# The first factor of a two-factor Fourier transform, on sums and differences of pairs of rows

## Chip, core and metric

The kernel runs on one core of a Trainium2 chip. The metric is device time in microseconds (us) of one execution, as the median of several. Engines are named as the profile does: PE (matmul), PEld (its weight loads), DVE (VectorE), ACT (ScalarE), POOL (GpSimd), SP (the queue that issues most DMAs).

## What is computed

The reference mixes a sequence in the frequency domain, and puts the result through a small network:

```python
X = np.fft.rfft(x, axis=1)                 # x: (8, 3008, 256)
y = np.fft.irfft(X * (filt_r + 1j * filt_i)[None], n=3008, axis=1)
h = y.reshape(24064, 256) @ w_in           # (256, 2048)
g = np.where(h > 0, h, np.exp(np.minimum(h, 0)) - 1)
out = g @ w_out                            # (2048, 256)
```

All is float32.

## The kernel before

The transform of length 3008 = 47 x 64 is split in two factors. A row of x has the number n = 47 n2 + n1, with n2 from 0 to 63 and n1 from 0 to 46. The first factor goes over n2 and yields, for each n1, the frequencies k2 from 0 to 31 (real input needs no more); a second, short factor goes over n1. Rows n1 = i and n1 = 47 - i are handled together, so i runs from 0 to 23 (`H`), in six chunks of four (`NXC`, `XC`).

For each of the 8 batches (b), these units follow each other:

- `x_load(b, c)` brings a chunk of x (partitions 0 to 63: n2 for n1 = i; 64 to 127: n2 for n1 = 47 - i) and a chunk of the table `ta` of cosines and sines, 128x128 for each i. The table has four groups p of 32 outputs: the real and imaginary parts of the sum over both n1.
- `a_unit(b, c)` is the first factor: four matmuls (L173), one for each i, with the 128x128 table as weights and 256 columns of x. Two of them fill one PSUM bank; ACT copies it out (L174).
- `z_write` puts the result into a scratch tensor z in DRAM (L186), `z_read(b, g)` fetches it in another order (L190, L191): the second factor needs i on partitions, for four k2 at a time.
- `b_unit(b, g)` does the second factor on four 64-wide tiles of the array (`tile_mm`, L218), multiplies by the filter on DVE, and adds on POOL. `bi_unit`, `y_write`, `y_read` and `n_unit` are the way back to rows of y; `n_unit` (L275) ends with combinations on DVE.
- The network follows in quads: one batch has 6 groups m of rows and 4 quarters q of the 2048 hidden columns, so 24 quads a batch and 192 in all. `up_steps` and `down_steps` do the two products with seven block products in place of eight, both for weights (prepared once by `w_convert`) and for data. `mm` is L323, the products of the down side L405, DVE's additions out of PSUM (`add`) L331.
- `c_unit` and `o_unit` combine and transpose the output, and 24 DMAs a group write it.

Each engine takes its instructions in the order in which they are written out. The network is the frame: a loop runs over the quads, with the steps of up (U) and down (D) interleaved by hand, and two places in each quad where the units of the transform are put in. Place 0 is in the middle, after the first seven steps, and place 1 at the end. The table `plan` says what goes where. Batch b's first factor runs during batch b-1's quads:

```python
for c, s in enumerate((0, 2, 3, 4, 6, 7)):
    at(t + s, 0, a_unit, b, c)
    nb, nxt = (b, c + XBUFS) if c + XBUFS < NXC else (b + 1, c + XBUFS - NXC)
    if nb < B:
        at(t + s, 0, x_load, nb, nxt)
    at(t + s, 0, z_write, b, c)
```

Here t is the first quad of batch b-1. Four PSUM banks (`bank`) rotate among all units; in the middle of a quad one of them is held by an open sum ("s"), and the next that is asked for is that of the products 7 and 4 ("d", written phd in the profile). DVE's addition of L331 reads that bank after product 7; product 4 is added to the same bank after that.

Batch 0 has no network to hide behind. It runs first, in a section of its own ("boot"), together with the fetch and conversion of the weights: x for all six chunks, the filter (`f_read_first`), 16 weight pieces (`w_fetch` on POOL's queue, `w_convert` on DVE and ACT). `wait_x` holds POOL's queue until a chunk of x has come.

Of the kernel before, what the change touches and what calls it, by code (L numbers as in the profile page):

```python
# [10 lines left out]
FP32 = mybir.dt.float32  # L11
U32 = mybir.dt.uint32
AXT = mybir.ActivationFunctionType
# [8 lines left out]
N = 3008  # L22
# [12 lines left out]
XBUFS = 4  # L35
FBUFS = 3
LO, HI = slice(0, 48), slice(64, 112)


def _make_tables():  # L40

    n2, k2 = np.arange(N2), np.arange(K2)
    ta, tn = np.zeros((P, H, P)), np.zeros((P, H, P))  # L50
    for i in range(H):
        for h in range(2):
            if h and i == 0:
                continue
            n1 = N1 - i if h else i
            th = 2 * np.pi * (((N1 * n2[:, None] + n1) * k2[None]) % N) / N
            c, s = np.cos(th), -np.sin(th)
            c[:, 0], s[:, 0] = 1.0, 1.0 - 2.0 * (n2 % 2)
            sign = -1.0 if h else 1.0
            r = slice(h * 64, h * 64 + 64)  # L60
            for p, v in enumerate((c, sign * s, s, sign * c)):
                ta[r, i, p * 32:p * 32 + 32] = v
                tn[p * 32:p * 32 + 32, i, r] = v.T
    i = np.arange(H)[:, None]
    gb, gr, gi = (np.zeros((P, 2, 64)) for _ in range(3))
    q = np.arange(N1)[None]
    th = 2 * np.pi * ((i * np.where(q < 24, q, 70 - q)) % N1) / N1
    c, s = np.cos(th), np.sin(th)
    sign = np.where(q < 24, 1.0, -1.0)
    gb[0:24, 0, :N1], gb[24:48, 0, :N1] = c, s  # L70
    gb[64:88, 0, :N1], gb[88:112, 0, :N1] = c * sign, -s * sign
    for o in (0, 64):
        gr[o:o + N1, 0, 0:24], gr[o:o + N1, 0, 24:48] = 2 / N * c.T, 2 / N * s.T
        gi[o:o + N1, 0, 0:24], gi[o:o + N1, 0, 24:48] = 2 / N * (c * sign).T, -2 / N * (s * sign).T
    k1 = np.arange(24)[None]
    t0 = 2 * np.pi * ((i * k1) % N1) / N1
    t3 = 2 * np.pi * ((i * (32 + 64 * k1)) % N) / N
    c0, s0, c3, s3 = np.cos(t0), np.sin(t0), np.cos(t3), np.sin(t3)
    gb[0:24, 1, 0:24], gb[24:48, 1, 24:48] = c0, c3
    gb[64:88, 1, 24:48], gb[88:112, 1, 0:24] = -s3, -s0  # L80

    m0, m3 = np.full((24, 1), 2 / N), np.full((24, 1), 2 / N)
    m0[0] = m3[23] = 1 / N
    s0[:, 0] = s3[:, 23] = 0.0
    gr[0:24, 1, 0:24], gr[24:48, 1, 24:48] = m0 * c0.T, m3 * c3.T
    gi[0:24, 1, 24:48], gi[24:48, 1, 0:24] = -m0 * s0.T, -m3 * s3.T
    return [t.astype(np.float32) for t in (ta, tn, gb, gr, gi)]
# [8 lines left out]
def kernel(  # L96
# [18 lines left out]
    glob = pool("glob", 1)  # L115
    xp = pool("xp", XBUFS)
    tap = pool("tap", XBUFS)
    tnp = pool("tnp", 2)
    t1p = pool("t1p", 3)
    t2p = pool("t2p", 2)  # L120
# [16 lines left out]
    junk = glob.tile([P, 1], FP32, name="junk")  # L137
    fd = fdp.tile([NG, 2, 48, 2, 2, D], FP32, name="fd")

    xs, tas, tns, t1s, t2s, ss, t3s, t4s, zs, yds, ys, g_of, po_of, cs_ = ({} for _ in range(14))  # L140

    def raw(src, row, ap, col=0):
        return bass.AP(tensor=src.tensor, offset=src.offset + row * D + col, ap=ap)
# [9 lines left out]


    def x_load(b, c, queue=nc.sync, place=None):
        t, w = place or (xp.tile([P, XC, D], FP32, tag="xc", name="xc"), tap.tile([P, XC, P], FP32, tag="ta", name="ta"))
        xs[b, c], tas[b, c] = t, w
        skip = 1 if c == 0 else 0
        if skip:
            nc.gpsimd.memset(t[64:P, 0, :], 0.0)  # L160
        queue.dma_start(w, ta_d[:, ts(c, XC), :])
        lo = b * N + c * XC
        nc.sync.dma_start(t[0:64], raw(x, lo, [[N1 * D, 64], [D, XC], [1, D]]))
        hi = b * N + N1 - c * XC - skip
        nc.sync.dma_start(t[64:P, skip:XC, :], raw(x, hi, [[N1 * D, 64], [-D, XC - skip], [1, D]]))

    def a_unit(b, c):
        t = t1s[b, c] = t1p.tile([P, XC, D], FP32, tag="t1", name="t1")
        xt, w = xs.pop((b, c)), tas.pop((b, c))
        for r in (0, 2):  # L170
            k, ps = bank("psa")
            for u in range(2):
                nc.tensor.matmul(ps[:, u, :], w[:, r + u, :], xt[:, r + u, :], start=True, stop=True)  # L173
            nc.scalar.activation(out=t[:, r:r + 2, :], in_=ps, func=AXT.Copy)  # L174
            banks.append(k)

    def z_write(b, c):  # L180
        if c == 0:
            zs[b] = zp.tile([96, K2 + 1, D], FP32, tag="z", name="z")
        t = t1s.pop((b, c))
        for p in range(4):
            r0 = p * H + c * XC
            nc.sync.dma_start(zs[b][r0:r0 + XC, 0:K2, :].rearrange("n k d -> k n d"), t[p * 32:p * 32 + 32, :, :])  # L186

    def z_read(b, g):
        t = t2s[b, g] = t2p.tile([P, 4, D], FP32, tag="t2", name="t2")
        nc.sync.dma_start(t[LO], zs[b][0:48, 4 * g:4 * g + 4, :])  # L190
        nc.sync.dma_start(t[HI], zs[b][48:96, 4 * g:4 * g + 4, :])  # L191

    def f_read(b, g):
        t = fbufs[(b * NG + g) % FBUFS]
# [3 lines left out]
    def f_read_first(t, a):  # L198
# [3 lines left out]
        for c, src in enumerate((filt_r, filt_i)):  # L202
# [7 lines left out]
                                            [[64 * D, n], [-4 * D, NG - g0], [1, D]]))  # L210
            if a == 0:
                nc.gpsimd.dma_start(t[24:48, 0, c, 0, :], raw(src, 32, [[64 * D, 24], [1, D]]))

    def tile_mm(ps, table, k, rhs, special):
        for u, w, v in ((0, 1, 1), (1, 1, 0)) if special else ((0, 2, 0),):
# [319 lines left out]
    with tc.manual_schedule():  # L537
# [3 lines left out]
        with tc.tile_pool(name="boot", bufs=1) as bp:  # L541
            ff = bp.tile([P, NG, 2, 2, D], FP32, name="ff")
            wbufs += [bp.tile([P, 2, 2, D], FP32, name="wb%d" % i) for i in range(2)]
            more = [(bp.tile([P, XC, D], FP32, name="xb%d" % i), bp.tile([P, XC, P], FP32, name="tb%d" % i))
                    for i in range(NXC - XBUFS)]

            def wait_x(c):

                nc.gpsimd.tensor_copy(out=junk[0:1], in_=xs[0, c][0:1, 0, 0:1])

            for k in range(2):
                w_fetch(k)
            for c in range(NXC):
                x_load(0, c, nc.scalar, more[c - XBUFS] if c >= XBUFS else None)
            nc.gpsimd.memset(ff, 0.0)
            for t, d in ((gb, gb_d), (gr, gr_d), (gi, gi_d)):
                nc.gpsimd.dma_start(t, d)
            w_convert(0)
            w_convert(1)
            wait_x(3)  # L560
            w_fetch(2)
            w_fetch(3)
            wait_x(5)
            for a in range(2):
                f_read_first(ff, a)
            for k in range(4, 7):
                w_fetch(k)
            for c in range(NXC):
                a_unit(0, c)
                z_write(0, c)  # L570
            for k in range(2, 6):
                w_convert(k)
                w_fetch(k + 5)
            z_read(0, 0)
            z_read(0, 1)
            for g in range(NG + 2):
                if g >= 2:
                    bi_unit(0, g - 2)
                if g < NG:
                    b_unit(0, g, ff[:, g])  # L580
                    if g + 2 < NG:
                        z_read(0, g + 2)
                if g >= 2:
                    y_write(0, g - 2)
                if g in CONVERTS:
                    w_convert(CONVERTS[g])
                if g == 1:
                    w_fetch(11)
                if g == 4:
                    w_fetch(12)  # L590
                if g in (5, 6):
                    x_load(1, g - 5)
# [26 lines left out]
        for b in range(B):  # L619
            t = (b - 1) * PER  # L620
            if b > 0:
                for c, s in enumerate((0, 2, 3, 4, 6, 7)):
                    at(t + s, 0, a_unit, b, c)
                    nb, nxt = (b, c + XBUFS) if c + XBUFS < NXC else (b + 1, c + XBUFS - NXC)
                    if nb < B:
                        at(t + s, 0, x_load, nb, nxt)
                    at(t + s, 0, z_write, b, c)
                for g in range(NG + 2):
                    s = t + 9 + g
                    if g >= 2:  # L630
                        at(s, 1, bi_unit, b, g - 2)
                    if g < NG:
                        at(s, 1, b_unit, b, g)
                    if g >= 2:
                        at(s, 1, y_write, b, g - 2)
                for g in range(NG):
                    s = t + 7 + g
                    at(s, 1, f_read, b, g)
                    at(s, 1, z_read, b, g)
            for m, (s, place) in enumerate(((20, 0), (25, 1), (29, 1), (32, 0), (36, 0), (40, 0))):  # L640
                if b > 0 or m > 0:
                    at(t + s - (1 if m == 0 else 2), 0, y_read, b, m)
                    at(t + s, place, n_unit, b, m)
                at(t + PER + 4 * m + 5, 0, c_unit, b, m)
                at(t + PER + 4 * m + 6, 0, o_unit, b, m)
# [54 lines left out]
```

## Time and profile before

| | |
|---|---|
| time, median of 3 | 2713.19 us (2712.85 to 2714.78) |
| span of the profiled execution | 2712.6 us, mean clock 0.978 |
| PE busy | 2618.7 us, 97% |
| DVE busy | 1809.0 us, 67% |
| L173, matmuls of `a_unit` (psa<-xc,ta; 16 more stand under psa<-xb,tb) | 368 records, 379 ns in the median |
| L174, copies of `a_unit` | 96, 584 ns mean |
| z<-t (L186) | 192 issues of 128 KB, 4.5 us to landing |
| t<-z (L190, L191) | 128 issues of 192 KB, 3.8 us to landing |
| ta<-ta_t on SP | 42 issues of 256 KB, 4.5 us to landing |

How to read it: busy time of PE is made of records that overlap in the pipe, so durations of groups are best taken from the start of one to the start of the next. A matmul statement in float32 appears as two records. DMA issues are named by destination and source. The time from issue to landing is the median.

### The profile page before, as it was taken

How to read it: one execution, taken by the hardware profiler on the slowest of the kernel's cores; microseconds unless marked ns; L12 is line 12 of the kernel's file. 1: busy time of each engine (PE TensorE's matmuls, PEld its weight loads, DVE VectorE, ACT ScalarE, POOL GpSimd, SP SyncE). 2: the span in 40 equal slices, each digit the busy share in tenths (PEclk: the TensorE clock that was granted, in tenths of full speed). 3: DMA queues.
4: the chain of work that ended last, by engine and by line, in shares of the span. 5: the costliest groups of instructions: out<-in, count | busy, mean ns of one | idle time of the engine just before them, and what ended most of it. 6: DMA issues, size and time to landing. Idle time of an engine off the chain costs nothing.

```text
span 2712.6 us, 35960 instructions
## 1 busy us (share of the span) xinstructions
PE 2618.7 (97%) x12992; PEld 2244.2 (83%) x12992; DVE 1809.0 (67%) x3147; ACT 1474.5 (54%) x2561; POOL 277.8 (10%) x325
## 2 busy tenths in 40 slices
PE   3689999999999999999999999999999999999998
PEld 1278878987899888998889887898789988899887
DVE  4866775667666676657765677666766667666765
ACT  2255555555555555555555555565555555555554
POOL 4311210002000120001200021000210012000000
PEclk7599999999999999999999999999999999999999
DMA  9655321434113431253313332143421233110010
GB/s 244 173 122 129 90 72 35 108 87 115 44 39 96 107 94 37 55 132 74 81 39 101 89 90 69 37 108 84 113 60 40 61 83 96 38 39 20 20 28 16
DMA packets 229424, 214.44 MB, mean 79 GB/s; under 512 B 131620, under 2 KB 192566, under 8 KB 229248
## 3 DMA queue, kind: packets, MB, share of 16 engines
q1 hardware_dynamic: 210592, 173.65, 25.7%
q0 software_dynamic: 17792, 36.93, 5.6%
q8 instruction: 103, 1.69, 0.3%
q10 hardware_dynamic: 864, 1.57, 0.2%
q14 instruction: 73, 0.60, 0.1%
HBM read 136.97 MB, written 78.12 MB: 79 GB/s over the span
## 4 chain that ended last, share of the span: by engine, by line
PE 95%; DMA 2%; DVE 1%; issue 1%; ACT 0%; POOL 0%; SPq 0%; DVEq 0%; ACTq 0%; POOLq 0%
PE po L405 42%; PE phs L323 24%; PE phd L323 12%; PE pha L323 6%; PE psn L275 3%; PE psa L173 3%; PE pva L218 2%; PE psr L218 2%; DMA wb<-in_moe_w_in_dram 1%; DMA tb<-ta_t 0%; DMA ff<-in_filt_i_dram 0%; PE pvb L218 0%; DMA ff<-in_filt_r_dram 0%; DMA xb<-in_x_dram 0%; DVE wm L488 0%
## 5 line engine op out<-in xcount | busy, mean ns | idle before, releaser
L405 PE MATMUL po<-g,wo 128*128 128x256 f32 (+1 forms) x5376 | 1293.4, 375 | 0.0
L405 PEld LDWEIGHTS po<-g,wo 128*128 128x128 f32 x5376 | 1019.5, 190 | 115.6
L334 ACT ACTIVATE g<-phs 128x512 f32<-128x512 f32 (+1 forms) x576 | 338.7, 588 | 844.5 <-PE phs L323 843.8
L331 DVE TENSOR_TENSOR g<-phd,g 128x512 f32<-128x512 f32 (+1 forms) x384 | 259.4, 675 | 537.9 <-ACT e L341 295.2
L341 ACT ACTIVATE e<-e 128x512 f32<-128x512 f32 (+1 forms) x768 | 477.0, 621 | 24.4
L323 PE MATMUL phs<-ys,wi 128*128 128x256 f32 (+1 forms) x1536 | 388.6, 375 | 11.2 <-ACT g L334 11.2
L323 PE MATMUL phs<-y,wi 128*128 128x256 f32 (+1 forms) x1536 | 394.8, 379 | 0.0
L345 DVE SCALAR_TENSOR_TENSOR g<-e,g 128x512 f32<-128x512 f32 (+1 forms) x576 | 386.6, 671 | 0.0
L340 ACT ACTIVATE e<-g 128x512 f32<-128x512 f32 (+1 forms) x576 | 352.9, 613 | 34.9 <-DVE g L331 30.1
L323 PEld LDWEIGHTS phs<-y,wi 128*128 128x128 f32 x1536 | 284.8, 190 | 82.9 <-ACT t L246 34.1
L323 PEld LDWEIGHTS phs<-ys,wi 128*128 128x128 f32 x1536 | 291.9, 190 | 45.5 <-ACT g L334 12.3
L345 DVE SCALAR_TENSOR_TENSOR g<-e,phs 128x512 f32<-128x512 f32 (+1 forms) x192 | 129.8, 676 | 138.6 <-ACT e L341 138.6
L235 POOL TENSOR_TENSOR sr<-sr,sp 128x512 f32<-128x512 f32 x64 | 81.1, 1267 | 1274.9 <-DVE sp L232 1274.9
L340 ACT ACTIVATE e<-phs 128x512 f32<-128x512 f32 (+1 forms) x192 | 112.9, 588 | 161.6 <-PE phs L323 161.6
L323 PE MATMUL phd<-ys,wi 128*128 128x256 f32 (+1 forms) x768 | 193.9, 375 | 0.5 <-DVE g L331 0.5
L323 PE MATMUL pha<-y,wi 128*128 128x256 f32 (+1 forms) x768 | 193.8, 375 | 0.0
L323 PE MATMUL phd<-y,wi 128*128 128x256 f32 (+1 forms) x768 | 193.7, 375 | 0.0
L323 PEld LDWEIGHTS phd<-ys,wi 128*128 128x128 f32 x768 | 145.7, 190 | 17.7 <-DVE g L331 1.3
L323 PEld LDWEIGHTS pha<-y,wi 128*128 128x128 f32 x768 | 145.8, 190 | 16.7 <-ACT y L277 0.2
L323 PEld LDWEIGHTS phd<-y,wi 128*128 128x128 f32 x768 | 145.8, 190 | 16.5
L385 DVE TENSOR_TENSOR g<-g,g 128x512 f32<-128x512 f32 (+1 forms) x192 | 130.7, 681 | 6.6
L382 DVE TENSOR_TENSOR g<-g,g 128x512 f32<-128x512 f32 (+1 forms) x192 | 130.7, 681 | 6.6
(102 smaller groups left out, 2313.2 us busy)
## 6 DMA issues: line engine op xcount, KB each, us to landing
z<-t SPq DMA_DIRECT2D x192, 128.0 KB, 4.5
t<-z SPq DMA_DIRECT2D x128, 192.0 KB, 3.8
yd<-t SPq DMA_DIRECT2D x128, 192.0 KB, 2.8
t<-yd SPq DMA_DIRECT2D x192, 128.0 KB, 3.7
xc<-in_x_dram SPq DMA_DIRECT2D x84, 256.0 KB, 5.2
f<-fd POOLq DMA_DIRECT2D x112, 192.0 KB, 3.7
out_dram<-o SPq DMA_DIRECT2D x640, 32.0 KB, 1.6
tn<-tn_t SPq DMA_DIRECT2D x48, 256.0 KB, 3.4
```

The lines of the kernel that those rows point to most:

```text
L173: nc.tensor.matmul(ps[:, u, :], w[:, r + u, :], xt[:, r + u, :], start=True, stop=True)
L218: nc.tensor.matmul(ps[:, u:u + w, :], table[k, v, :], rhs[k, u:u + w, :], start=True, stop=True)
L275: nc.tensor.matmul(ps[:, ts(q, P)], t[:, i - 4 * m, ds(dh * P, P)], w[:, i - 4 * m, :], start=True, stop=True)
L323: nc.tensor.matmul(ps[:, a, 0:h], w_in[q][:, COMBO[n], a, :], y[n], start=start and a == 0, stop=True, skip_group_check=True)
L331: nc.vector.tensor_tensor(out=g[o], in0=i0, in1=i1, op=ALU.add)
L334: nc.scalar.activation(out=g[o], in_=i0, func=AXT.Copy)
L340: nc.scalar.activation(out=e, in_=src, func=AXT.Relu, scale=-1.0)
L341: nc.scalar.activation(out=e, in_=e, func=AXT.Exp, scale=-1.0)
L345: nc.vector.scalar_tensor_tensor(out=g[n], in0=es[n], scalar=1.0, in1=src, op0=ALU.subtract, op1=ALU.max)
L382: nc.vector.tensor_tensor(out=b12, in0=b22, in1=b12, op=ALU.subtract)
L385: nc.vector.tensor_tensor(out=g["t4"], in0=g["b21"], in1=g["t2"], op=ALU.subtract)
L405: nc.tensor.matmul(po[i][:, u, 0:h], w_out[q][:, COMBO[n], a, :], g[n][:, a, :], start=q == 0 and a == 0 and n in (1, 3, 6, 4), stop=True, ...
```

## The change

A cosine or sine of the angle 2 pi (47 n2 + n1) k2 / 3008 keeps its value when n2 grows by 32 if k2 is even, and changes its sign if k2 is odd. So even k2 need only x[n2] + x[n2 + 32], and odd k2 only x[n2] - x[n2 + 32], with n2 from 0 to 31. The change has DVE make these sums and differences (`x_unit`), and lets the first factor run on a contraction of 32 rows for each n1. A 64x64 tile then holds both n1 of one i, and all four groups p for the 16 even, or the 16 odd, k2. Four such tiles fill the array: two i on the upper and lower rows, even and odd k2 on the left and right columns. Eight matmuls of 256 columns do a chunk.

Around it, the layout of x changes (partitions: 32 n2 of n1 = i, 32 n2 of 47 - i, for two halves of the chunk; the free dimension holds n2 and n2 + 32), the table halves, z has one row for each i with 128 lines in the order (p, k2) and one of padding, so that `z_write` takes two DMAs in place of four and `z_read` four in place of two. `x_unit` goes into place 0 of the quad before its `a_unit`. In the boot section the first factor stands ahead of the later weight fetches in the text, and the first two `w_convert` come after chunks 0 and 2.

```diff
+    tb = ta.reshape(2, 2, 32, NXC, 2, 2, 4, 16, 2)[:, 0].transpose(3, 0, 1, 2, 4, 7, 5, 6)
+    ta = np.ascontiguousarray(tb).reshape(P, H // 2, P)
...
+    sdp = pool("sdp", 2)
...
     def x_load(b, c, queue=nc.sync, place=None):
...
-        queue.dma_start(w, ta_d[:, ts(c, XC), :])
-        lo = b * N + c * XC
-        nc.sync.dma_start(t[0:64], raw(x, lo, [[N1 * D, 64], [D, XC], [1, D]]))
-        hi = b * N + N1 - c * XC - skip
-        nc.sync.dma_start(t[64:P, skip:XC, :], raw(x, hi, [[N1 * D, 64], [-D, XC - skip], [1, D]]))
+        queue.dma_start(w, ta_d[:, 2 * c:2 * c + 2, :])
+        for h in range(2):
+            i = XC * c + 2 * h
+            r = slice(64 * h, 64 * h + 32)
+            nc.sync.dma_start(t[r].rearrange("p k u d -> p k (u d)"),
+                              raw(x, b * N + i, [[N1 * D, 32], [32 * N1 * D, 2], [1, 2 * D]]))
+            r = slice(64 * h + 32, 64 * h + 64)
+            for u in range(2):
+                if i + u == 0:
+                    nc.gpsimd.memset(t[r, :, 0, :], 0.0)
+                else:
+                    nc.sync.dma_start(t[r, :, u, :],
+                                      raw(x, b * N + N1 - i - u, [[N1 * D, 32], [32 * N1 * D, 2], [1, D]]))
+
+    def x_unit(b, c):
+        t = xs[b, c]
+        u = sds[b, c] = sdp.tile([P, 2, D], FP32, tag="sd", name="sd")
+        nc.vector.tensor_tensor(out=u, in0=t[:, 0], in1=t[:, 1], op=ALU.add)
+        nc.vector.tensor_tensor(out=t[:, 1], in0=t[:, 0], in1=t[:, 1], op=ALU.subtract)
...
     def a_unit(b, c):
...
-        for r in (0, 2):
-            k, ps = bank("psa")
-            for u in range(2):
-                nc.tensor.matmul(ps[:, u, :], w[:, r + u, :], xt[:, r + u, :], start=True, stop=True)
-            nc.scalar.activation(out=t[:, r:r + 2, :], in_=ps, func=AXT.Copy)
-            banks.append(k)
+        (i0, p0), (i1, p1) = (bank("psa") for _ in range(2))
+        for u in range(2):
+            for o, src in ((0, sm), (64, xt[:, 1])):
+                for ps, r in zip((p0, p1), HALVES):
+                    nc.tensor.matmul(ps[o:o + 64, u, :], w[r, u, o:o + 64], src[r, u, :], start=True, stop=True)
+        nc.scalar.activation(out=t[:, 0:2, :], in_=p0, func=AXT.Copy)
+        nc.scalar.activation(out=t[:, 2:4, :], in_=p1, func=AXT.Copy)
+        banks.extend((i0, i1))
...
-            zs[b] = zp.tile([96, K2 + 1, D], FP32, tag="z", name="z")
+            zs[b] = zp.tile([H, 4 * K2 + 1, D], FP32, tag="z", name="z")
...
-        for p in range(4):
-            r0 = p * H + c * XC
-            nc.sync.dma_start(zs[b][r0:r0 + XC, 0:K2, :].rearrange("n k d -> k n d"), t[p * 32:p * 32 + 32, :, :])
+        z = zs[b][XC * c:XC * c + XC, 0:4 * K2, :].rearrange("i (q r) d -> r q i d", r=2)
+        for r in range(2):
+            nc.sync.dma_start(z[r], t[HALVES[r]])
...
-        nc.sync.dma_start(t[LO], zs[b][0:48, 4 * g:4 * g + 4, :])
-        nc.sync.dma_start(t[HI], zs[b][48:96, 4 * g:4 * g + 4, :])
+        for p, r in enumerate((0, 24, 64, 88)):
+            k = p * K2 + 4 * g
+            nc.sync.dma_start(t[r:r + 24].rearrange("i u d -> i (u d)"), zs[b][:, k:k + 4, :].rearrange("i u d -> i (u d)"))
...
-            w_convert(0)
-            w_convert(1)
...
+            for c in range(NXC):
+                x_unit(0, c)
+                a_unit(0, c)
+                z_write(0, c)
+                if c in (0, 2):
+                    w_convert(c // 2)
             for k in range(4, 7):
                 w_fetch(k)
-            for c in range(NXC):
-                a_unit(0, c)
-                z_write(0, c)
...
                 for c, s in enumerate((0, 2, 3, 4, 6, 7)):
+                    at(t + s - 1, 0, x_unit, b, c)
                     at(t + s, 0, a_unit, b, c)
```

More of the change, by code (lines that the diff above doesn't have):

```diff
@@ L37 @@
 LO, HI = slice(0, 48), slice(64, 112)
+HALVES = slice(0, 64), slice(64, 128)
 def _make_tables():
@@ L138 @@
     fd = fdp.tile([NG, 2, 48, 2, 2, D], FP32, name="fd")
-    xs, tas, tns, t1s, t2s, ss, t3s, t4s, zs, yds, ys, g_of, po_of, cs_ = ({} for _ in range(14))
+    xs, tas, tns, t1s, t2s, ss, t3s, t4s, zs, yds, ys, g_of, po_of, cs_, sds = ({} for _ in range(15))
     def raw(src, row, ap, col=0):
@@ L155, in x_load @@
     def x_load(b, c, queue=nc.sync, place=None):
-        t, w = place or (xp.tile([P, XC, D], FP32, tag="xc", name="xc"), tap.tile([P, XC, P], FP32, tag="ta", name="ta"))
+        t, w = place or (xp.tile([P, 2, 2, D], FP32, tag="xc", name="xc"), tap.tile([P, 2, P], FP32, tag="ta", name="ta"))
         xs[b, c], tas[b, c] = t, w
-        skip = 1 if c == 0 else 0
-        if skip:
-            nc.gpsimd.memset(t[64:P, 0, :], 0.0)
-        queue.dma_start(w, ta_d[:, ts(c, XC), :])
-        lo = b * N + c * XC
@@ L167, in a_unit @@
+    def x_unit(b, c):
[3 more added lines that the diff above has]
+        nc.vector.tensor_tensor(out=t[:, 1], in0=t[:, 0], in1=t[:, 1], op=ALU.subtract)
     def a_unit(b, c):
         t = t1s[b, c] = t1p.tile([P, XC, D], FP32, tag="t1", name="t1")
-        xt, w = xs.pop((b, c)), tas.pop((b, c))
-        for r in (0, 2):
-            k, ps = bank("psa")
-            for u in range(2):
-                nc.tensor.matmul(ps[:, u, :], w[:, r + u, :], xt[:, r + u, :], start=True, stop=True)
-            nc.scalar.activation(out=t[:, r:r + 2, :], in_=ps, func=AXT.Copy)
-            banks.append(k)
+        xt, w, sm = xs.pop((b, c)), tas.pop((b, c)), sds.pop((b, c))
+        (i0, p0), (i1, p1) = (bank("psa") for _ in range(2))
[6 more added lines that the diff above has]
+        banks.extend((i0, i1))
@@ L543 @@
             wbufs += [bp.tile([P, 2, 2, D], FP32, name="wb%d" % i) for i in range(2)]
-            more = [(bp.tile([P, XC, D], FP32, name="xb%d" % i), bp.tile([P, XC, P], FP32, name="tb%d" % i))
+            more = [(bp.tile([P, 2, 2, D], FP32, name="xb%d" % i), bp.tile([P, 2, P], FP32, name="tb%d" % i))
                     for i in range(NXC - XBUFS)]
             def wait_x(c):
-                nc.gpsimd.tensor_copy(out=junk[0:1], in_=xs[0, c][0:1, 0, 0:1])
+                nc.gpsimd.tensor_copy(out=junk[0:1], in_=xs[0, c][0:1, 0, 0, 0:1])
             for k in range(2):
```

## The prediction

> **What bounds the kernel now.** I read the page from the top: busy shares and slices, then the chain that ended last, then busy time by stretch.
>
> ```profile
> PE 2618.7 (97%) x12992; PEld 2244.2 (83%) x12992; DVE 1809.0 (67%) x3147; ACT 1474.5 (54%) x2561; POOL 277.8 (10%) x325
> PE   3689999999999999999999999999999999999998
> DVE  4866775667666676657765677666766667666765
> DMA  9655321434113431253313332143421233110010
> PE 95%; DMA 2%; DVE 1%; issue 1%; ACT 0%; POOL 0%; SPq 0%; DVEq 0%; ACTq 0%; POOLq 0%
> ```
>
> ```profile
> 0.00:68.00 68.00, 20.61 (x60) 13.24 (x60) 28.02 (x55) 15.70 (x26) 30.91 (x49) 0.74 1.03 244
> 68.00:136.00 68.00, 45.41 (x152) 16.13 (x149) 58.13 (x103) 17.70 (x32) 25.85 (x26) 0.51 0.64 174
> 272.00:2644.00 2372.00, 2372.00 (x11915) 2052.27 (x11914) 1593.76 (x2757) 1335.66 (x2320) 198.09 (x225) 1.00 0.28 71
> ```
>
> The columns of the second block are the stretch, its length, busy us of PE, PEld, DVE, ACT and POOL, the clock, the DMA share and GB/s. From 272 to 2644 us PE is busy for 2372.00 of 2372 us at full clock. There every nanosecond taken from PE comes off the total, and nothing else does, as long as no new wait opens. The first 68 us are another kernel: PE 20.6 us, DMA share 1.03, so transfers set the pace; from 68 to 136 DVE is busy for 58 of 68 us.
>
> Next, how long PE is held by one `a_unit`, and by the unit in this kernel that already has the shape of the new one, `b_unit`. From the timeline of PE (start, length, line, group):
>
> ```profile
> 521.80 1.89 PE L173 MATMUL psa<-xc,ta 128*128 128x256 f32 x8
> 523.53 0.92 PE L405 MATMUL po<-g,wo 128*128 128x224 f32 x4
> ...
> 608.20 1.89 PE L405 MATMUL po<-g,wo 128*128 128x256 f32 x8
> 610.01 0.64 PE L218 MATMUL psr<-t,gb 48*64 48x512 f32 x1
> 610.02 0.64 PE L218 MATMUL psi<-t,gb 48*64 48x512 f32 x1
> ...
> 611.03 1.13 PE L323 MATMUL phs<-y,wi 128*128 128x256 f32 x4
> 612.00 1.03 PE L323 MATMUL pha<-y,wi 128*128 128x256 f32 x4
> 612.87 1.03 PE L405 MATMUL po<-g,wo 128*128 128x256 f32 x4
> ```
>
> One matmul statement leaves two records. Lengths overlap (the pipe), so I go by starts: the four statements of `a_unit` take 523.53-521.80 = 1.73 us, 0.43 us for 256 columns. Four full-array records (two statements) step by 612.87-612.00 = 0.87.
>
> `b_unit` has four statements on 64-column tiles, two row halves by two column halves, 512 columns each. One after the other that is 4 x 0.87 = 3.5 us. The group before should have ended at 608.20+1.73 = 609.93; the group after starts at 611.03 and is 0.10 longer than usual (0.97 against 0.87). So it costs 1.10+0.10 = 1.20 us: the four tiles run together in 0.87, and 0.33 us goes into leaving and re-entering the full array. The `b_unit` of g = 0, where half of the tiles get two statements of 256 columns, comes out at 1.22 by the same sum (594.88+1.73 to 597.73, plus 0.11).
>
> Last, the gap of DVE in which the new work must fit, from its timeline in the quad that has `c_unit` too:
>
> ```profile
> 535.09 0.38 DVE L421 TENSOR_TENSOR c<-k,k 128x224 f32<-128x224 f32 x1
> 537.19 0.69 DVE L331 TENSOR_TENSOR g<-phd,g 128x512 f32<-128x512 f32 x1 [1.72 <-ACT e L341]
> 537.79 0.68 DVE L345 SCALAR_TENSOR_TENSOR g<-e,g 128x512 f32<-128x512 f32 x1
> ```
>
> and the table loads of the first 68 us, by queue (packets, MB, share of 16 engines):
>
> ```profile
> q10 hardware_dynamic: 864, 1.57, 9.1%
> ```
>
> **What the Trainium skill says.** TensorEngine Tiling (Array Packing), Key Properties: tiles of a 64x64 split load and multiply independently of each other, and changing the tiling mode drains the engine. The trace agrees: four tiles in 0.87 us, and 0.33 us for the change of mode. The same page, Gotcha 1: different row tiles must write to different PSUM banks; the new code does so (p0 for the upper half, p1 for the lower). VectorE: DVE Perf Modes, the perf-mode tier table: fp32 `tensor_tensor` has no fast mode. The trace has 0.68 us for 128x512, and 0.60 from start to start. DMA: Bandwidth & Descriptors, on why a DMA increments its semaphore by 16: a transfer is spread over the largest number up to 16 that divides its slowest dimension. By that rule a read of 24 rows uses 12 engines where 48 rows used 16; no view here shows it.
>
> **The change, part by part.**
>
> 1. *Matmuls of `a_unit`.* Four full-array statements of 256 columns become eight 64x64 ones, in two rounds of four different tiles. If the rounds run as in `b_unit`: 2 x 0.43 = 0.87 us of streaming, plus 0.33 for the mode, plus some 0.02 for more statements, so 1.22 us instead of 1.73. Saved: 0.51 us. Bounds: 1.03 us if half of the switch hides (0.70 saved), 1.40 if the sixteen short weight loads (129 ns each at L218) don't all hide (0.33 saved). I take 1.22 because L218 is the same engine, tile shape, type and neighbours. 48 units exist; six belong to the start, and the first of batch 1 (138.5 us) is followed by a wait of 9.36 us of PE that DVE's weight conversion sets. That leaves 41 on the path: 41 x 0.51 = 20.9 us.
>
> 2. *`x_unit` on DVE.* 48 pairs of 128x512 fp32 operations, 0.60 us apart: 1.2 us a pair (1.36 by lengths). It is queued in the middle of a quad, one quad (13 us) before its `a_unit`, so PE does not wait for it directly. Behind it in DVE's queue stands the addition of L331 out of phd, which PE needs before it may add product 4 into the same bank. DVE stands idle there for 5.76 us in a quad without extras and 1.72 us in the fullest one of steady state (1.43 in the narrowest that I found); all hold 1.2 us. If it were late by a little, PE has two more groups (0.87 each) between product 7 and product 4. On the path: 0.
>
> 3. *Transfers of steady state.* `x_load` goes from three to seven issues (six for the first), the table from 256 to 128 KB, `z_write` from four to two, `z_read` from two to four. SP issues at 0.3 to 0.6 us each; per batch this is some 24-12+16 = 28 more, about 13 us in a batch of over 300 us. x is asked for three quads or more before use, and the last `z_write` has two quads before its `b_unit`. DMA share is 0.28 in this stretch. On the path: 0.
>
> 4. *ACT.* Two copies of 128x512 a unit as before; the first becomes ready later, by under a microsecond, while ACT is still at the exponentials queued before it. On the path: 0.
>
> 5. *The start.* Six table loads shrink by half: 9.1% of 68 us is 6.2 us of all 16 engines, so 3.1 us of a saturated stretch are freed. Against it: 35 instead of 12 x issues on SP (some 0.42 us each, 15 us, where the old ones with their stalls took until 18.7 us), 1.2 us for sums before each matmul, and reads of z over fewer engines. The packets of x halve from 4 to 2 KB in one part, with no more bytes. The two early weight conversions move behind the first sums, into a time in which DVE had gaps of 8.84 and 14.44 us. The chain goes x, filter loads, weight fetch, conversion, so it should move up nearly by what is freed. I take -2.5 us, bounds -5 and +6.
>
> Sum: 2713.2 - 20.9 - 2.5 = 2689.8, say 2690.
>
> **The rivals.**
>
> A. *The start gives something back.* Many small issues on a saturated SP queue, and z read over 12 engines. For it: SP stalls between x loads already (issues at 2.07 and 5.52). Against: fewer bytes, half the z issues. 2713.2-20.9+6 = 2698.
>
> B. *The switch hides more than in `b_unit`.* 1.03 us a unit, start -5: 2713.2-28.7-5 = 2680. Against: all `b_unit`s that I measured pay the 0.33.
>
> C. *Tiles pair up but don't run four at a time*, for instance because four different moving operands are read at once: 2 x 0.87 + 0.33 = 2.07 us, 0.34 more than now, 41 x 0.34 = 14 us: about 2725 with the gain at the start. Slower than before. Against: `b_unit` reads two moving tiles on each row half too.
>
> D. *DVE becomes late.* If the addition out of phd slips past its slack by half a microsecond in each of the 41 quads, the gain is gone: 2711 to 2714. Against: the gaps above.
>
> **How the numbers follow.** Forecast 2690: 0.63. A: 0.15. B: 0.11. C: 0.06. D: 0.05. The range 2681 to 2700 takes in the forecast with the bounds of a unit from 1.1 to 1.3 us, all of A and nearly all of B; C and D stay out. Faster by over 0.2% (below 2707.8): forecast, A, B, and a part of D, 0.91; within: 0.02; slower: 0.07.
>
> **What would show it.** In the changed profile PE stays at full busy time from 272 us to the end of steady state; between the groups around an `a_unit` some 1.2 us pass, with eight tile records starting within some tens of nanoseconds and the second eight about 0.2 to 0.4 us later; `x_unit` shows 96 operations at 0.68 us, with the wait of L331 for phd shorter by 1.2 us, and no PE wait for DVE. The first `b_unit` starts near 62 instead of 64.0 us. It is wrong if the tile records start one pair after the other, if PE shows waits for DVE L331, or if the first `n_unit` (130.76 us) starts later than before.

## The result, and the profile after

The changed kernel takes 2698.05 us (median of 4, 2697.19 to 2699.75), the kernel before beside it 2713.72 us (4 runs, 2712.85 to 2714.78): ratio 0.9943, 95% interval 0.9926 to 0.9960. It is faster by 15.7 us where 23.4 were forecast, and lands on the number of rival A, 2698, though in part by luck (below). A second measurement in the middle of the experiments (below, the changed kernel again) gave 2698.47 us, ratio 0.9941 (0.9927 to 0.9954).

From the page of the changed kernel, the busy time of each engine:

```profile
PE 2593.4 (96%) x13376; PEld 2196.4 (81%) x13376; DVE 1870.0 (69%) x3243; ACT 1474.7 (55%) x2561; POOL 279.9 (10%) x325
```

PE lost 25.3 us of busy time, and DVE gained 61.0 us with 96 operations more. By stretch (start and end, length, busy us of PE, PEld, DVE, ACT and POOL, clock, DMA share, GB/s):

```profile
0.00:68.00 68.00, 12.90 (x97) 8.52 (x98) 32.08 (x64) 14.58 (x25) 30.49 (x48) 0.75 0.91 232
68.00:136.00 68.00, 44.02 (x146) 14.38 (x145) 58.07 (x101) 16.75 (x30) 25.92 (x26) 0.50 0.56 157
272.00:2630.00 2358.00, 2358.00 (x12222) 2016.81 (x12221) 1643.22 (x2832) 1339.52 (x2325) 199.19 (x225) 1.00 0.28 70
```

From 272 us on PE is as full as before, at full clock, so the frame of the prediction holds. In the first 68 us the DMA share is 0.91, where it was 1.03. Now one `a_unit` in the timeline of PE (start, length, group):

```profile
509.83 0.92 PE L426 MATMUL po<-g,wo 128*128 128x224 f32 x4
510.59 0.92 PE L344 MATMUL phs<-ys,wi 128*128 128x224 f32 x4
511.44 0.43 PE L194 MATMUL psa<-sd,ta 64*64 64x256 f32 x2
511.45 0.43 PE L194 MATMUL psa<-xc,ta 64*64 64x256 f32 x2
511.71 0.38 PE L194 MATMUL psa<-sd,ta 64*64 64x256 f32 x2
...
512.15 0.38 PE L194 MATMUL psa<-xc,ta 64*64 64x256 f32 x2
512.47 1.02 PE L426 MATMUL po<-g,wo 128*128 128x224 f32 x4
513.33 0.92 PE L344 MATMUL phd<-y,wi 128*128 128x224 f32 x4
```

Such a group of 224 columns holds PE for 0.76 us (510.59-509.83). The next group could have started at 511.35; it starts at 512.47 and takes 0.10 longer (513.33-512.47 = 0.86). So the unit costs 1.12+0.10 = 1.22 us, the number of the forecast. Its sixteen records start within 0.71 us (511.44 to 512.15), in four rounds of four, where the prediction had two rounds of eight.

To split the result I use one fixed point: a wait of PE for ACT of 9.4 us at the end of the weight conversions, which both kernels have once. It ends at the second line of each pair here (before, then after); the first line of each is a short wait just ahead of it:

```profile
137.63 1.02 PE L323 MATMUL phs<-ys,wi 128*128 128x224 f32 x4 [0.63 <-ACT g L334]
154.58 1.86 PE L323 MATMUL phs<-ys,wi 128*128 128x224 f32 x4 [9.36 <-ACT g L334]
141.60 1.02 PE L344 MATMUL phs<-ys,wi 128*128 128x224 f32 x4 [0.63 <-ACT g L355]
158.05 1.86 PE L344 MATMUL phs<-ys,wi 128*128 128x224 f32 x4 [9.37 <-ACT g L355]
```

From this release to the end: before 2712.6-154.58 = 2558.0 us, after 2697.7-158.05 = 2539.65. Steady state gained 18.4 us; all before the release lost 18.4-15.7, that is 2.7 us. The release itself comes 3.5 us later (158.05-154.58), and the trace of the second measurement gives 18.9 and 3.4 by the same two sums, so the loss is about 3 us.

Between the two waits the changed kernel gains: 16.95 us before, 16.45 after. The first `a_unit` of batch 1 stands there, and the chain that ended last runs through it. So this unit saves its 0.50 us too, which the prediction had put at nothing because a long wait follows, and what comes ahead of it lost some 3.2 us.

The waits of PE from 141 to 2630 us, in the changed kernel (engine, what waits, for what: us in total, times, longest):

```profile
PE phs L344 <- ACT g L355: 11.2, 3, 9.4
PE phd L344 <- DVE g L352: 1.8, 1, 1.8
```

The second was 0.5 us before. DVE's timeline shows where it is, in quad 5, while the second batch's first factor runs:

```profile
215.56 0.91 DVE L690 MEMSET f<- 128x1024 f32 x1 [0.16 <-issue]
...
217.95 0.38 DVE L442 TENSOR_TENSOR c<-k,k 128x224 f32<-128x224 f32 x1
218.25 0.69 DVE L182 TENSOR_TENSOR sd<-xc 128x512 f32<-128x512 f32 x1
218.97 0.69 DVE L183 TENSOR_TENSOR xc<-xc 128x512 f32<-128x512 f32 x1
219.58 0.69 DVE L352 TENSOR_TENSOR g<-phd,g 128x512 f32<-128x512 f32 x1
```

and PE's line for the group that waits, with the idle time and its releaser in brackets, before and after:

```profile
216.01 1.13 PE L323 MATMUL phd<-ys,wi 128*128 128x256 f32 x4 [0.48 <-DVE g L331]
220.32 1.13 PE L344 MATMUL phd<-ys,wi 128*128 128x256 f32 x4 [1.82 <-DVE g L352]
```

Three memsets, four operations of `c_unit` and the pair of `x_unit` stand in one queue with hardly a gap, and the addition of L352 that PE needs comes behind them.

At the start, the chain of waits of the changed kernel up to the first `b_unit` (start, length, what; `SPq` is an issue by SP):

```profile
12.13 0.31 SPq L176
...
12.96 0.42 SPq L169
...
22.37 0.43 SPq L176
22.84 6.09 DMA xb<-in_x_dram
...
29.06 0.17 POOL junk L570
...
33.13 11.07 DMA ff<-in_filt_i_dram
...
47.36 13.09 DMA z<-t
...
61.16 6.42 DMA t<-z
```

and that of the kernel before:

```profile
4.19 13.34 DMA tb<-ta_t
...
17.54 6.96 DMA xb<-in_x_dram
...
24.62 0.17 POOL junk L549
...
28.86 13.24 DMA ff<-in_filt_i_dram
...
51.30 8.03 DMA wb<-in_moe_w_in_dram
```

Before, the chain runs through transfers. After, 10.7 us of it are SP issuing x loads one after the other, 0.47 us from one to the next; the last chunk arrives at 29.06 us in place of 24.62, and GpSimd's fetches of the filter stand behind it. The chains go on differently, too, to the first filter product of `b_unit` on DVE. Before, the way is a fetch of weights (51.30+8.03 = 59.33) and the conversions behind it, which leave DVE at 68.45 us; the product follows at 69.04. After, the way is a write and a read of z (47.36+13.09, then 61.16+6.42 = 67.58) and the matmuls of `b_unit`; the product follows at 72.36. The first `n_unit` starts at 133.91 us, not 130.76.

### The profile page after: what moved, and what is told of

It is laid out like the page before. It is cut to its first block, busy times and chain, and to the rows that moved or that the text cites. A ratio compares the mean times of both kernels' runs of the same rounds, so it can differ in the third digit from the quotient of the medians.

```text
span 2697.7 us, 37154 instructions
## 1 busy us (share of the span) xinstructions
PE 2593.4 (96%) x13376; PEld 2196.4 (81%) x13376; DVE 1870.0 (69%) x3243; ACT 1474.7 (55%) x2561; POOL 279.9 (10%) x325
## 3 DMA queue, kind: packets, MB, share of 16 engines
q1 hardware_dynamic: 216096, 168.15, 25.3%
## 4 chain that ended last, share of the span: by engine, by line
PE 94%; DMA 2%; DVE 2%; issue 1%; SPq 0%; ACT 0%; POOL 0%; ACTq 0%; DVEq 0%; POOLq 0%
PE po L426 42%; PE phs L344 25%; PE phd L344 12%; PE pha L344 6%; PE psn L296 3%; PE pva L239 2%; PE psr L239 2%; PE psa L194 2%; DMA z<-t 0%; DMA ff<-in_filt_i_dram 0%; DMA ta<-ta_t 0%; PE pvb L239 0%; SPq L176 0%; DMA t<-z 0%; DMA xb<-in_x_dram 0%
## 5 line engine op out<-in xcount | busy, mean ns | idle before, releaser
L352 DVE TENSOR_TENSOR g<-phd,g 128x512 f32<-128x512 f32 (+1 forms) x384 | 259.6, 676 | 462.8 <-ACT e L362 277.8
```

The costliest lines, as they stand in the source:

```text
L352: nc.vector.tensor_tensor(out=g[o], in0=i0, in1=i1, op=ALU.add)
```

## Experiments

The ratios are against the kernel before, measured beside each run.

**1. Only the tiles undone.** The loads, the sums, the half tables and the scratch lines stay; the matmuls are full-array again. Even and odd k2 are not kept apart in it, so it doesn't compute the transform.

```diff
-            for o, src in ((0, sm), (64, xt[:, 1])):
-                for ps, r in zip((p0, p1), HALVES):
-                    nc.tensor.matmul(ps[o:o + 64, u, :], w[r, u, o:o + 64], src[r, u, :], start=True, stop=True)
+            for ps, src in ((p0, sm), (p1, xt[:, 1])):
+                nc.tensor.matmul(ps[:, u, :], w[:, u, :], src[:, u, :], start=True, stop=True)
```

> The changed kernel with its sums and differences, tables of half the size, loads and scratch lines, but with the first factor's matmuls over the full 128 partitions again: four a unit, of 128x128 weights over 256 columns. This leaves out part of the computation: even and odd k2 are not kept apart, so the output is not the transform. Theory (the tiles bring the whole gain in the steady stretch, 0.51 us times 41 units on the path): 2698.3 + 20.9 = 2719, so 5 us above the kernel before, which is what the rest of the change costs (x_unit, more issues, the start). Rival (the loads, tables or scratch lines bring a part of the gain): less than 2711. Rival (the tiles bring more than that and the rest of the change costs more): above 2724.

Measured: 2719.46 us (before 2714.53), ratio 1.0020 (1.0012 to 1.0028). One unit in the timeline of PE:

```profile
503.15 0.59 PE L193 MATMUL psa<-sd,ta 128*128 128x256 f32 x2
503.58 0.59 PE L193 MATMUL psa<-xc,ta 128*128 128x256 f32 x2
...
504.88 0.92 PE L425 MATMUL po<-g,wo 128*128 128x224 f32 x4
```

It takes 504.88-503.15 = 1.73 us again, and the total is 21.0 us over that of the changed kernel (2698.47), where 41 x 0.51 = 20.9 was forecast. So the tiles bring the whole gain. Between the two waits of the fixed point 16.95 us pass again (142.09 to 159.04), as before the change. The rest of the change costs 4.9 us: from the release of the 9.4 us wait (159.04 us) to the end (2719.0) 2560.0 us pass, 2.0 more than before, and 2.9 come before the release. That agrees with the changed kernel's 2.7.

**2. `x_unit` with its sum made three times** (batches 1 to 7).

```diff
         nc.vector.tensor_tensor(out=u, in0=t[:, 0], in1=t[:, 1], op=ALU.add)
+        if b > 0:
+            nc.vector.tensor_tensor(out=u, in0=t[:, 0], in1=t[:, 1], op=ALU.add)
+            nc.vector.tensor_tensor(out=u, in0=t[:, 0], in1=t[:, 1], op=ALU.add)
```

> The changed kernel with the sum of x_unit made three times for the seven later batches: 1.3 to 1.4 us more of DVE for each of 42 units, 57 us in all. Theory (DVE has a gap of 1.4 us or more before it answers TensorE, except in the quads with a c_unit or a memset, where 0.39 us is left beside some 1.7 us of TensorE's own slack): the time grows by 0 to 8 us, the wait of TensorE for the DVE addition of group d appears in the quads with x_unit and c_unit, and nowhere else. Rival (DVE is on the path wherever x_unit runs, and the 1.2 us of x_unit are paid each time): 30 to 57 us more, so over 2728.

Measured: 2709.25 us, ratio 0.9981 (0.9974 to 0.9988): 10.8 us more than the changed kernel, for 57.6 us more of DVE (1927.6 against 1870.0). The waits of PE from 141 to 2630 us:

```profile
PE phs L347 <- ACT g L358: 10.6, 2, 9.4
PE phd L347 <- DVE g L355: 7.2, 8, 3.3
```

The wait for DVE is the one that theory names, eight times, and accounts for 5.4 us of the growth. More shows when the weight loads (PEld) wait for the same addition, here and in the changed kernel:

```profile
PEld phd L347 <- DVE g L355: 13.8, 16, 3.7
PEld phd L344 <- DVE g L352: 2.9, 3, 2.2
```

From one quad's first `pha` group to the next, the two kernels differ in the quads that have both `x_unit` and `c_unit`: by 0.80 us in quad 1 and 0.37 us in quad 5 of the 24, in each of the six later batches, and by 3.1 us in the quad 5 shown above, 1.7 of them at a lower clock (last section). That is 10.1 of the 10.8 us. So DVE's slack takes in nearly all of one `x_unit`, but not of twice that: a fifth of the added work is paid, a little more than expected.

**3. The first factors in pairs.** `x_unit` for both chunks at place 0, and both `a_unit` calls at place 1, of quads 2, 4 and 6.

```diff
-                for c, s in enumerate((0, 2, 3, 4, 6, 7)):
-                    at(t + s - 1, 0, x_unit, b, c)
-                    at(t + s, 0, a_unit, b, c)
+                for c, s in enumerate((2, 2, 4, 4, 6, 6)):
+                    at(t + s, 0, x_unit, b, c)
+                    if c % 2 == 0:
+                        continue
+                    at(t + s, 1, a_unit, b, c - 1)
+                    at(t + s, 1, a_unit, b, c)
...
```

> The changed kernel with the first factors of steady state in pairs: two a_units back to back at the end of quads 2, 4 and 6, both x_units in the middle of the same quad. If a change of tile mode costs 0.33 us a time, a pair pays it once: 3 x 7 = 21 fewer, 7 us under e5; and no x_unit stands in quad 5 behind the memsets, so the wait of 1.8 us of PE there goes: together 2689 to 2691. If the cost of 0.33 us belongs to each unit (weight loads that do not hide), only the 1.8 us go: 2696. If four banks in a row make PE wait for ACT's copies: slower than e5 by up to 20 us.

Measured: 2694.47 us, ratio 0.9924 (0.9912 to 0.9936), 4.0 us less than the changed kernel. The pair in the timeline of PE:

```profile
503.29 1.68 PE L426 MATMUL po<-g,wo 128*128 128x224 f32 x8
504.89 0.43 PE L194 MATMUL psa<-sd,ta 64*64 64x256 f32 x2
...
506.78 1.02 PE L344 MATMUL phs<-y,wi 128*128 128x224 f32 x4
507.64 0.92 PE L344 MATMUL pha<-y,wi 128*128 128x224 f32 x4
```

It should have been over at 503.29+1.51 = 504.80; with the 0.10 of the next group it costs 2.08 us, not 2 x 1.22 = 2.44. The 0.36 us saved are one change of tiling mode. From the release (157.23 us) to the end (2692.4) 2535.2 us pass, 4.5 less than in the changed kernel. Three terms make 4.3: the first unit of batch 1 has moved behind the release (21 x 2.08 = 43.7 us against 41 x 1.22 = 50.0, so 6.3 less); the wait for DVE did not go, but moved to 182 us, where two `x_unit` stand behind a conversion and the combinations of an `n_unit`, and is 2.1 us long (0.3 more); and for some 4 us after it the granted clock is lower (1.7 more, last section).

**4. The start.** Eight runs ask which part of the change loses time there. First two ways to make it better in the changed kernel. The loads of the upper 64 partitions of x issued from ACT's queue:

```diff
+        def xq(h):
+            return queue if h else nc.sync
...
-            nc.sync.dma_start(t[r].rearrange("p k u d -> p k (u d)"),
+            xq(h).dma_start(t[r].rearrange("p k u d -> p k (u d)"),
```

> The changed kernel, with the x loads of the start (batch 0 only) issued from two queues: the lower 64 partitions by SP as before, the upper 64 by ACT, behind its table loads. SP then has 17 instead of 35 x issues at the start; bytes and order are the same. Theory issues (SP's rate of issue sets when x arrives, DMA share was 0.60 between 10 and 20 us): last x some 4 to 8 us earlier, first b_unit at 64 to 65 instead of 67.7 us, time 2694 to 2696. Rival reads (z is read over fewer engines) and rival order (conversions stand between the sums): no change, 2697 to 2699.

And the order of the boot section as before the change (two conversions ahead of the sums, three weight fetches ahead of the first factors):

```diff
+            w_convert(0)
+            w_convert(1)
             wait_x(3)
...
+            for k in range(4, 7):
+                w_fetch(k)
             for c in range(NXC):
                 x_unit(0, c)
                 a_unit(0, c)
                 z_write(0, c)
-                if c in (0, 2):
-                    w_convert(c // 2)
-            for k in range(4, 7):
-                w_fetch(k)
```

> The changed kernel with the start in the old order: both early weight conversions ahead of all sums, and all six first factors after the fetches 4 to 6 in the text. Rival order: the sums no longer wait behind conversions, first b_unit 2 to 4 us earlier, 2694 to 2696. Theory issues: x does not come earlier, so within 1 us of 2698.

Measured: 2699.01 us (ratio 0.9943, 0.9928 to 0.9957) and 2698.93 us (0.9944, 0.9929 to 0.9959). Neither differs from the changed kernel. With two queues the DMA share between 10 and 20 us rose from 0.60 to 0.92, so SP's issues are what kept the DMA engines idle there; but ACT was still issuing at 25 us, made its first copy at 26.6 us, and its last at 52.4 in place of 46.1 (start).

Then parts of the change in the kernel before, one at a time. The loads of x of batch 0 cut into six issues a chunk, with packets of the old size:

```diff
+            for k in range(2):
+                nc.sync.dma_start(t[32 * k:32 * k + 32], raw(x, lo + 32 * k * N1, [[N1 * D, 32], [D, XC], [1, D]]))
...
```

> The kernel before, with nothing but the x loads of batch 0 (and the two of batch 1 that use places set aside or not, b > 0 stays as it was) cut into six issues a chunk instead of two, same bytes. Theory issues: x later by 4 us or more, the first b_unit 2 to 4 us later than 64.0, time 2715 to 2717. Rivals: no change, 2713 to 2714.

`z_read` in four reads of 24 rows:

```diff
-        nc.sync.dma_start(t[LO], zs[b][0:48, 4 * g:4 * g + 4, :])
-        nc.sync.dma_start(t[HI], zs[b][48:96, 4 * g:4 * g + 4, :])
+        for p, r in enumerate((0, 24, 64, 88)):
+            nc.sync.dma_start(t[r:r + 24], zs[b][24 * p:24 * p + 24, 4 * g:4 * g + 4, :])
```

> The kernel before, with z_read in four issues of 24 rows instead of two of 48, nothing else. Rival reads: landing of z is longer by a fifth to a third, the first b_unit 1 to 3 us later, time 2714 to 2716. Theory issues: no change in the steady state, under 1 us at the start, 2713 to 2714.

The whole new order of the scratch lines, with two writes a chunk and four reads:

```diff
-            zs[b] = zp.tile([96, K2 + 1, D], FP32, tag="z", name="z")
+            zs[b] = zp.tile([H, 4 * K2 + 1, D], FP32, tag="z", name="z")
...
```

> The kernel before with the new layout of z alone: one row for each i with lines (p, k2), two writes of 64 partitions a chunk, four reads of 24 rows a group. Rival layout (writes of 256 KB in this order land later and hold t1 longer): first b_unit 2 to 4 us later than 64.0, time 2 to 4 us over before. Theories two limits and traffic: within 1 us of before.

Measured: 2714.77 us (1.0002, 0.9994 to 1.0011), 2715.05 us (1.0004, 0.9995 to 1.0013) and 2715.49 us (1.0006, 0.9998 to 1.0014). The issues do delay the last chunk of x, to 27.23 us from 24.62, but the fetch of weight piece 4 starts at 51.24 us as before (51.30), and the total doesn't move. By the medians none of the three makes up the loss. But their intervals reach to 3.0, 3.5 and 3.8 us, so a loss of about 3 us is not excluded for any of them, least of all for the reads and the scratch lines: in the profiled executions of these two the first filter product comes at 71.75 and 71.48 us, not 69.04. Single executions count for little here, though: among six runs with one and the same start, the changed kernel's, it comes between 70.85 and 72.36.

The changed kernel again, beside the two improvements together:

> The changed kernel itself, once more, as the base of this group. Expected 2697 to 2700.

> The changed kernel with both edits of the start at once: x for the upper partitions issued by ACT's queue in batch 0, and the old order (conversions first, first factors after the fetches). Theory two limits (either one alone leaves the other in place, so both had to go): last x and first z write 5 to 8 us earlier, first b_unit near 62 to 64, time 2.5 to 5 us under e5. Rival traffic (the transfers of filter, z and weights share the DMA engines from 25 us on, so earlier z writes end no earlier): within 1 us of e5.

Measured: 2698.47 us, and 2702.93 us (0.9959, 0.9947 to 0.9971). Together they lose 4.5 us, where theory had a gain: ACT issues until 26.4 us, its first conversion starts at 27.7, the first sums wait for it, and the first write of z is issued at 40.24 us instead of 29.13.

Last, GpSimd's own fetches released two chunks earlier:

```diff
-            wait_x(3)
+            wait_x(1)
...
-            wait_x(5)
+            wait_x(3)
```

> The changed kernel, with GpSimd released for its own fetches two chunks of x earlier (the waits on chunks 3 and 5 become waits on chunks 1 and 3). Theory: at the start of the changed kernel SyncE's 35 issues, not the 16 DMA engines, feed the transfers (busy share 0.60 between 10 and 20 us, where the kernel before had 1.08), so the filter and weight fetches can fill the idle share: the share in 10 to 20 us rises above 0.8, the fetch of weight piece 4 starts before 51 us instead of 53, the first b_unit comes at 65 us or earlier instead of 67.5, and the total is 2 to 4 us below the changed kernel's, some 2695. Rival (what delays the start is the path of x itself through DVE, TensorE, ACT and z, and not the room on the DMA engines): earlier fetches take room from x, the z writes start no earlier than 28 us, and the time is 2698 within 1 us, or a little above.

Measured: 2698.32 us (0.9939, 0.9926 to 0.9951), no difference. Its chain of waits:

```profile
22.57 0.22 POOL junk L570
...
49.05 7.30 DMA wb<-in_moe_w_in_dram
...
71.17 0.68 DVE sr L251
```

The share from 10 to 20 us rose to 0.82, and weight piece 4 was fetched at 49.05 us, 4.4 us earlier than in the changed kernel (53.40). But the first filter product of `b_unit` starts at 71.17, only 1.2 us before the changed kernel's 72.36: the conversions behind that fetch now end last, for DVE runs from 55.3 us up to the product with hardly a gap, while the first `b_unit` starts at 65.99 us in place of 67.71. The idle room on the DMA engines is real, and filling it isn't enough.

**5. Pairs, and the first of them inside the wait.** Batch 1's first two `x_unit` go ahead of the first hidden layer's DVE work (quad -1), its first two `a_unit` to the end of quad 0, ahead of the conversions.

```diff
+        plan[0, 1] = first + plan[0, 1]
...
+                    early = b == 1 and c < 2
+                    s = 0 if early else s
+                    at(t + s - (1 if early else 0), 0, x_unit, b, c)
...
```

> The kernel with paired units, but the first pair of the second batch is made earlier: its two x_unit calls before the first hidden layer's DVE work, its two a_unit calls at the end of that batch's quad 0, ahead of the weight conversions. There TensorE waits 9.4 us for ScalarE anyway, behind DVE's conversions. Theory: the pair costs nothing on the path any more (2.1 us), and the wait of 2.1 us of TensorE for the DVE addition of group d at 182 us goes, since no x_unit stands ahead of it: 2694.5 - 2.1 - 2.1 = 2690, within 1.5 us. Rival (the 9.4 us wait is moved by what is put ahead of it, since the DVE chain that releases it begins later): no gain, 2694 to 2696, and the wait ends later than 157.5 us by as much as the pair takes.

Measured: 2687.00 us (before 2714.04), ratio 0.9898 (0.9882 to 0.9915): 11.5 us less than the changed kernel, and 7.5 less than plain pairs, where 4.2 were forecast. PE at the end of quad 0:

```profile
147.03 0.38 PE L194 MATMUL psa<-xc,ta 64*64 64x256 f32 x2
148.03 1.02 PE L344 MATMUL phs<-y,wi 128*128 128x224 f32 x4 [0.62 <-ACT t L195]
...
157.27 1.86 PE L344 MATMUL phs<-ys,wi 128*128 128x224 f32 x4 [6.71 <-ACT g L355]
```

The wait shrank from 9.4 to 6.7 us and ends at 157.27, where it ended at 157.23 in the run with plain pairs: it took in most of the pair (counted from the short wait ahead of it, as in the fixed point, the release comes 0.7 us later than with plain pairs: 16.06 against 15.38 us). No wait for DVE is left after it. From the release to the end 2529.2 us pass, 10.4 less than in the changed kernel (2539.65). 41 x 1.22 - 20 x 2.08 = 8.4 and the wait of 1.8 make 10.2. Against plain pairs it is 6.0 less (2535.2 there): the pair 2.1, the wait 2.1, and the 1.7 of lower clock that followed that wait. What is left of the 7.5 lies ahead of the release, where single executions vary.

## Why the prediction was half right

- **Step 1, the matmuls: right but for one unit.** 1.22 us a unit forecast, 1.22 in the trace, and 21.0 us between the kernels with and without the tiles against 20.9. From one quad's first `pha` group to the next, each of the 36 quads with a unit in the six later batches is 0.50 or 0.51 us shorter than before, and no other quad there has changed by as much as 0.12. What the Trainium skill says in TensorEngine Tiling (Array Packing), Key Properties, that tiles work independently and that a change of tiling mode drains the engine, fits both halves: the sixteen records start within 0.71 us, where four full-array statements take 1.73, and 0.36 us are saved where two units share one change. Pricing it by the `b_unit` of the same kernel was enough. Rivals B and C fall. What the step had wrong is the count: the first unit of batch 1 is on the path (0.50 us from the short wait to the release), so there are 42.
- **Step 2, DVE: right for all units but one.** The 1.2 us fit into the gap ahead of L352 nearly everywhere, and rival D is out. The step failed in one quad. There a PE wait of 0.48 us for DVE stood already, and the pair of `x_unit` came on top in full: 1.82 us. I measured the gaps of DVE and looked past the one place where the gap was negative.
- **Steps 3 and 4: nothing on the path, as forecast.** PE has no wait for a transfer, and none for ACT beyond those it had, from 272 us on.
- **Step 5, the start: wrong in sign.** -2.5 us forecast, about +3 measured (2.7 to 3.5). The step's premise failed: that the start is a saturated stretch, in which freed bytes are freed time. After the change SP's issues pace the loads (10.7 us of the chain), the DMA share between 10 and 20 us falls from 1.08 to 0.60, and the 3.1 us freed by the half table meet engines that stand idle for part of the time. What turns this into time is not known. By their medians the issues alone, the reads alone, the scratch lines alone, the order of the boot section and the free room on the DMA engines each leave the total where it was within about 1.5 us, but the intervals are wider than that. It may take several of them together, or the sums ahead of each matmul, or the smaller packets of x; the last two weren't tried alone. One reason why single edits do little is seen: two paths end close together ahead of the first filter product, DVE's weight conversions (at 68.45 us before, 70.39 after) and z with the matmuls of `b_unit` (which start at 64.00 and 67.71). Shortening one leaves the other, as the last run on the start shows. The reads of 24 rows would by the Trainium skill (DMA: Bandwidth & Descriptors, on why a DMA increments its semaphore by 16) go over 12 engines; alone they move the median by 0.2 us, and no view shows the engines that they use. That the loss lies ahead of the first filter product is shown by the two traces: from there to the first combination of `n_unit` both kernels take 64.5 us.

Of the three signs of being wrong that the prediction named, two came true: PE waits for DVE's addition, and the first `n_unit` starts later.

Of the 7.7 us that the forecast promised too much (23.4 against 15.7), 5.2 are all that comes ahead of the release (2.5+2.7), 1.3 the one wait (1.82-0.48), and 1.2 remain. Of these some 0.8 are clock: in the 8 us after the release the mean granted clock was 0.76 before and 0.66 after, which is 1.9 and 2.7 us of full clock lost; in the trace of the second measurement it is 2.1, and the stretch to the end is 0.5 us shorter.

Rival A named the right place, but its number fits by luck: it had 6 us at the start and nothing after it, where some 3 us lie at the start and the rest is the wait and the clock. Its reason, many issues on one queue, is seen in the chain, but isn't shown to be the cause.

## What to carry to other kernels

- Price a new form of matmul by a unit of the same kernel that has it already, with the change of mode counted; then put such units side by side, so that the change is paid once.
- Before adding work to an engine with "slack", look for a wait on it that is already there: a gap that is mostly wide is no help in the one place where it is negative. And work for the engine that sets the pace costs little where that engine waits anyway, if nothing that ends the wait stands behind it: the pair ahead of the conversions cost 0.7 us in place of 2.08, but a unit ahead of what starts them puts off the end of the wait (16.95 us before, 16.45 after, 15.38 with no unit there).
- A high DMA share at the start may be due to a few large issues. Count the issues as well as the bytes before calling a saved byte a saved nanosecond.

## What the hardware did unexpectedly

- Some waits of PE cost more than their length, because the granted clock is lower after them. After the wait of 9.4 us it was 0.50 for 3.8 us in the kernel before, and for 5.5 us in the changed kernel. A wait of 2.08 us (pairs, 182.37 us) was followed by 0.63 from 183 to 185 us and 0.51 from 185 to 187, 1.7 us of full clock lost: eight records that take 1.68 us elsewhere took 2.89. A wait of 3.26 us (sum three times, 221.21 us) was followed by 0.59 from 222 to 224 us and 0.56 from 224 to 226. A wait of 1.82 us in the changed kernel (220.32 us) was followed by none of this, clock 1.00. In the case of 2.08 us, waits of 9.5 and 1.2 us had gone before within 30 us; whether these matter isn't known.
- ACT's instructions stand behind DMA issues in its own queue: with 18 loads of x and six of the table there (loads of x from two queues), its first copy came at 26.6 us.
